# The second layer's sums of weights and of x^T: from GpSimd to the vector engine

## The chip, the cores and the metric

One NeuronCore of a Trainium2 chip runs the whole program. The metric is the device time of one execution in microseconds; the kernel before has a median of 953.41 us over three runs (953.21 to 955.58). Engines are called as the profile calls them: PE is TensorE's matrix multiply, PEld its weight load, DVE the vector engine, ACT the scalar engine, POOL GpSimd, SP the queue that issues the transfers.

## The reference, cut to what matters

```python
attn_out = windowed_attention(q, k, v)                 # 4 x 8 heads, 576 positions, width 64
x = attn_out.transpose(0, 2, 1, 3).reshape(2304, 512)
x = rational(x @ moe_w_in) @ moe_w_out                 # layer 1: 512 -> 2048 -> 512
h = x @ moe2_w_in                                      # layer 2: 512 -> 2048
g = where(h > 0, h, exp(min(h, 0)) - 1)
return g @ moe2_w_out                                  # 2048 -> 512
```

All is float32. The change touches layer 2 alone.

## The kernel before

The kernel keeps x transposed (tile `xT`) and runs attention, layer 1 and layer 2 one after the other. Layer 2 starts at about 551 us of the span. Each float32 operand of a product is split into a high part, rounded to the matmul's format by ACT (`hi_w`, `hi_op`, lines 870 and 905), and a low part, which DVE makes as the difference (`lo`, line 875); each product is three passes.

Layer 2 goes over three groups J of 768 tokens, and in each over 8 steps of 256 columns of d_ff: 24 steps q. Within a step, h of 2 x 2 blocks is made by seven block products instead of eight. They are called b11, b21, t2, t3, t1, t4 and b22 (`product`, line 918), and they need sums of blocks: four sums of weight blocks (`sum_w`, line 848, four instructions of 128x256 that read the tile `two` and write the two tiles `s`) and four sums of blocks of x^T (`sum_x`, line 896, two instructions of 128x384 each). DVE adds the seven products up into the four blocks of h (`added`, line 974, which reads the product m from PSUM), ACT and DVE make g from each block (lines 980, 984, 989, 1006 and 875), and PE multiplies g of the step before by w_out (`gemm2`, line 934). On PE a step is b11, b21, G0, t2, t3, G1, t1, G2, t4, b22, G3, where G are the four second products.

Sums of weights are made once, in the first group, for w = 0 to 7 (w is the step they belong to), stored in DRAM by SP (`keep_sums`, line 853) and loaded again in the other groups. w = 0 and w = 1 are summed by DVE, w = 2 to 7 by POOL. The two tiles `s` are the same for all w, so the sums of one w wait until the stores of the last one have landed and its low parts are made. The sums of x^T for J = 0 are made by DVE during layer 1; those for J = 1 and J = 2 by POOL, over the x rows of the group before.

Layer 2's order is not written by hand. `step` notes for each piece of work its engine, an estimated cost and what it needs; `in_order` lays the pieces out with those costs, by due times counted back from PE's fixed order, counting a transfer as landed 3500 ns behind its issue cost (1200 for a load of weight blocks), and every engine then runs its pieces in that order. The estimates of before are 3500 ns for a set of four weight sums on POOL, 1400 ns for one on DVE, and 2300 ns for two sums of x^T on POOL. An engine's real start is set by semaphores: POOL, with nothing else to do, starts a sum as soon as its data are there.

Of the kernel before, what the change touches and what calls it, by code (L numbers as in the profile page):

```python
# [44 lines left out]
def kernel(  # L45
# [13 lines left out]
    nc = tc.nc  # L59
# [150 lines left out]
    def cv_tile(shape, dtype, name, n=None):  # L210
        n = next(n_cv) if n is None else n
        return cv.tile(shape, dtype, tag=f"cv{n}", name=f"{name}{n}")
# [480 lines left out]
    def experts():  # L693
# [47 lines left out]
        OPS, XO, sums, G, sq, kept, low_part = {}, {}, {}, {}, {}, {}, {}  # L741
# [56 lines left out]
        def raw_ones(q):  # L798

            return [e for e in range(2) if q < NP2 and ("wo", KF + 2 * q + e) not in early_ones]  # L800

        def load_raw(q, e):
            key = ("wo", KF + 2 * q + e)
            SLOT[key] = SETS[q % 3]["EF"[e]]
            load_w(key)

        def load_wi(q):
            two[q] = t = at(q, "C", [P, 2, PC], F32, "two")
            for e in range(2):
                nc.sync.dma_start(out=t[:, e], in_=joined["wi", KF + q % NP2 * 2 + e])  # L810
# [6 lines left out]
        def load_wo(q, e):  # L817
            nc.sync.dma_start(out=both(e), in_=joined["wo", KF + q % NP2 * 2 + e])

        def scale_wo(q, e):  # L820
            key = ("wo", KF + 2 * q + e)
            T32[key] = both(e)
            nc.scalar.activation(out=both(e), in_=words(key)[1].bitcast(F32), func=AF.Copy, scale=2.0 ** -112)

        def join_wo(q, e):
            key = ("wo", KF + 2 * q + e)
            conv_shift(key)
            conv_or(key)
            conv_sign(key)
            del RAW[key]  # L830

        def keep_wo(q, e):
            key = ("wo", KF + 2 * q + e)
            joined[key] = d = dram.tile([P, PC], F32, name="joined_%s_%d" % key)
            nc.sync.dma_start(out=d, in_=T32[key])

        def sum_w(q, eng=nc.gpsimd, ns=range(4)):
            w = two[q]
            a11, a12, a21, a22 = [w[:, e, h * HC:(h + 1) * HC] for e in range(2) for h in range(2)]
            if 0 in ns:  # L840
                sq[q] = [cv_tile([P, 2, HC], F32, "s", n) for n in range(2)]
            s = sq[q]
            for n in ns:
                x, y, op = (
                    (a21, a22, ALU.add), (s[0][:, 0], a11, ALU.subtract), (a11, a21, ALU.subtract),
                    (a12, s[0][:, 1], ALU.subtract),
                )[n]
                eng.tensor_tensor(out=s[n // 2][:, n % 2], in0=x, in1=y, op=op)

        def keep_sums(w):  # L850
            kept[w] = [dram.tile([P, PC], F32, name=f"sums_{w}_{n}") for n in range(2)]
            for d, t in zip(kept[w], sq[w]):
                nc.sync.dma_start(out=d, in_=t.rearrange("p s c -> p (s c)"))

        def load_sums(w):
            sq[w] = [cv_tile([P, 2, HC], F32, "s", n) for n in range(2)]
            for d, t in zip(kept[w % NP2], sq[w]):
                nc.sync.dma_start(out=t.rearrange("p s c -> p (s c)"), in_=d)

        def hi_w(q, x):  # L860
            if x in "CD":
                src = sq[q]["CD".index(x)].rearrange("p s c -> p (s c)")
            elif x == "B":
                src = two[q][:, 1, HC:PC]
            elif x == "A":
                src = two[q][:, 0]
            else:
                src = pair[0][:, "EF".index(x)]
            OPS[q, x] = t = at(q, x, [P, 2, HC if x == "B" else PC], F32R, "op")
            nc.scalar.activation(out=t[:, 0], in_=src, func=AF.Copy)  # L870
            low_part[q, x] = (t[:, 1], src, t[:, 0])

        def lo(key, eng=nc.vector):
            out, src, hi = low_part.pop(key)
            eng.tensor_tensor(out=out, in0=src, in1=hi.bitcast(F32), op=ALU.subtract)  # L875

        def x_row(J, k, T):
            c0 = (2 * J + T) * TB
            return xT[:, k, c0:c0 + TB]

        def sum_x(J, n, eng=nc.gpsimd, ks=range(2)):

            if 0 not in ks:
                pass
            elif J == 0:
                nm = "_".join(map(str, t_slots[n]))
                t = wpool.tile([P, 2, TB], F32, tag=nm, name=f"t_{nm}")
                sums[J, n] = [t[:, k] for k in range(2)]
            else:
                sums[J, n] = [x_row(J - 1, k + 2 * (n // 2), n % 2) for k in range(2)]  # L890
            for k in ks:
                b11, b21, b12, b22 = [x_row(J, k + 2 * i, T) for T in range(2) for i in range(2)]
                x, y = (
                    (b12, b11), (b22, sums[J, 0][k]), (b22, b12), (b21, sums[J, min(n, 1)][k]),
                )[n]
                eng.tensor_tensor(out=sums[J, n][k], in0=x, in1=y, op=ALU.subtract)
# [63 lines left out]
        def step(key, engine, cost, fn, *needs):  # L960
            todo[key] = (engine, cost, fn, needs)
            if engine == "PE":
                pe_order.append(key)
# [71 lines left out]
        def weight_steps(w):  # L1035

            def part(x, cost_hi, cost_lo, *needs):
                step((w, "hi", x), "ACT", cost_hi, lambda: hi_w(w, x), *needs)
                step((w, "lo", x), "DVE", cost_lo, lambda: lo((w, x)), (w, "hi", x))

            if w == 0:
                step((w, "kept"), "SP", 1200, lambda: keep_sums(w))
            else:
                out_gone = [(w - 2, "out", T, t) for T in range(2) for t in range(NTT)]
                if w > 1:
                    step((w, "load"), "SP", 1200, lambda: load_wi(w), (w - 3, "t1"), (w - 3, "t2"))
                gone = [(w - 1, "lo", "C"), (w - 1, "lo", "D")]
                if w >= NP2:
                    step((w, "sum"), "SP", 1200, lambda: load_sums(w), *gone)
                else:  # L1050
                    eng, cost, at = (nc.vector, 1400, "DVE") if w == 1 else (nc.gpsimd, 3500, "POOL")
                    step((w, "sum"), at, cost, lambda: sum_w(w, eng), (w, "load"), *gone, (w - 1, "kept"))
                    step((w, "kept"), "SP", 1200, lambda: keep_sums(w), (w, "sum"))
                part("A", 520, 600, (w, "load"), (w - 3, "b11"), (w - 3, "b21"), *out_gone)
                part("B", 300, 340, (w, "load"), (w - 3, "t4"), *out_gone)
                part("C", 520, 600, (w, "sum"), (w, "lo", "A"), (w, "lo", "B"))
                part("D", 520, 600, (w, "sum"), (w - 3, "t3"), (w - 3, "b22"), *out_gone)
            for e, x in enumerate("EF"):
                gone = [(w - 2, "G", n) for n in ((0, 3), (1, 2))[e]]
                if e in raw_ones(w):  # L1060
                    if w > 0:
                        step((w, "raw", x), "SP", 600, lambda e=e: load_raw(w, e), *gone)
                    step((w, "scale", x), "ACT", 570, lambda e=e: scale_wo(w, e), (w, "raw", x), (w - 1, "lo", x),
                         (w - 1, "keep", x))
                    step((w, "words", x), "DVE", 1600, lambda e=e: join_wo(w, e), (w, "scale", x))
                    step((w, "keep", x), "SP", 600, lambda e=e: keep_wo(w, e), (w, "words", x))
                else:
                    step((w, "words", x), "SP", 600, lambda e=e: load_wo(w, e), (w - 1, "lo", x),
                         (w - 1, "keep", x), (w - NP2, "keep", x))
                part(x, 520, 600, (w, "words", x), *gone)  # L1070
# [9 lines left out]
        def x_sums(J, q):  # L1080

            used = [("xlo", J - 1, nm, k) for nm in ORDER for k in range(2)]
            for n in range(4):
                step(("sum", J, n), "POOL", 2300, lambda n=n: sum_x(J, n), *used, (q - 4 + n, "b11"),
                     *[("sum", J, i) for i in range(n)])

        def second(q):
# [32 lines left out]
            if p == NP2 - 1 and q + 1 < NQ:  # L1120
                x_sums(q // NP2 + 1, q)
                x_steps(q // NP2 + 1, ORDER, q)
# [165 lines left out]
```

## Time and profile before

| | value |
|---|---|
| median of 3 runs | 953.41 us (953.21 to 955.58) |
| profiled execution, its own time | 951.87 us |
| its span | 950.2 us |
| PE busy | 920.9 us (97%) |
| DVE busy | 818.8 us (86%) |
| ACT busy | 745.1 us (78%) |
| POOL busy | 248.6 us (26%) |

Busy times are sums over the whole span; the three stages have different limits, so a share of the span says little about layer 2. Matmul ends are modelled, so that the start of a product is a safer mark than its busy time. DVE instructions overlap a little: the next one starts some 0.08 us before the last one's recorded end, so that the distance from start to start is what an instruction costs a full engine.

### The profile page before, as it was taken

What the parts mean: (1) busy time and instruction counts of PE and PEld (TensorE: products, weight loads), DVE (VectorE), ACT (ScalarE), POOL (GpSimd) and SP (SyncE); (2) the same over time, 40 slices, a digit from 0 to 9 for tenths busy, and PEclk for the clock granted to TensorE, in tenths of its full rate; (3) what the DMA queues carried; (4) which work ended last, traced back from release to release, by engine and by line L of the source; (5) the groups of instructions that cost most, each with busy time, mean ns of one, the idle gap of its engine ahead of it and who ended that gap; (6) DMA issues with size and microseconds to landing.
All of it is one profiled execution on the core that took longest, in us unless ns stands there. A gap on an engine that the chain in (4) does not pass through costs nothing.

```text
span 950.2 us, 16856 instructions
## 1 busy us (share of the span) xinstructions
PE 920.9 (97%) x5494; PEld 839.0 (88%) x5494; DVE 818.8 (86%) x1890; ACT 745.1 (78%) x1635; POOL 248.6 (26%) x312
## 2 busy tenths in 40 slices
PE   7999998999999999999999999999999999999998
PEld 5766767999999999999999988878889898989897
DVE  5999998999999999999999999899987678787653
ACT  4999999889889889889888986656777566766553
POOL 4777772122222222222222225350310000000000
PEclk8999999999999999999999999999999999999999
DMA  6899943011231222222210034434344332443201
GB/s 165 207 236 242 235 135 95 1 34 34 84 100 51 84 83 68 84 67 86 82 46 28 26 120 125 142 122 152 104 140 149 100 100 68 162 141 96 78 1 67
DMA packets 112424, 98.36 MB, mean 104 GB/s; under 512 B 62800, under 2 KB 86096, under 8 KB 112336
## 3 DMA queue, kind: packets, MB, share of 16 engines
q1 hardware_dynamic: 112336, 97.29, 35.1%
q8 instruction: 43, 0.70, 0.3%
q14 instruction: 45, 0.37, 0.1%
HBM read 79.96 MB, written 17.30 MB: 102 GB/s over the span
## 4 chain that ended last, share of the span: by engine, by line
PE 63%; DVE 18%; ACT 14%; issue 4%; DMA 1%; POOL 0%; SPq 0%; DVEq 0%; ACTq 0%; POOLq 0%
PE acc L934 17%; PE h L260 15%; PE acc L705 15%; PE m L918 14%; ACT pT L441 2%; ACT pr_wo L515 2%; ACT pr_wi L515 2%; DVE ghi L301 2%; DVE qq L304 1%; DVE ee L322 1%; DVE ee L318 1%; DVE qq L313 1%; DVE h L321 1%; DVE op_wi L875 1%; DVE op_wo L875 1%
## 5 line engine op out<-in xcount | busy, mean ns | idle before, releaser
L260 PE MATMUL h<-xs,w_wi 128*128 128x384 f32 x1152 | 218.1, 335 | 1.3 <-ACT xs L235 0.8
L260 PEld LDWEIGHTS h<-xs,w_wi 128*128 128x128 f32 x1152 | 200.4, 188 | 4.2 <-DVE xs L236 2.4
L705 PE MATMUL acc<-ghi,w_wo 128*128 128x384 f32 x768 | 195.0, 334 | 0.0
L319 POOL TENSOR_TENSOR glo<-ee,rr 128x384 fp32r<-128x384 f32 x92 | 93.5, 1016 | 315.8 <-DVE ee L318 160.9
L705 PEld LDWEIGHTS acc<-ghi,w_wo 128*128 128x128 f32 x768 | 138.7, 188 | 0.0
L705 PE MATMUL acc<-glo,w_wo 128*128 128x384 f32 x384 | 128.7, 335 | 0.9 <-DVE glo L319 0.5
L934 PE MATMUL acc<-op_wo,ghi 128*128 128x512 f32 x288 | 89.6, 392 | 0.0
L307 ACT ACTIVATE rr<-qq,c_q 128x384 f32<-128x384 f32 x96 | 59.3, 618 | 38.5 <-DVE qq L304 37.7
L918 PE MATMUL m<-xo_wo,op_wi 128*128 128x384 f32 x336 | 77.1, 337 | 7.2 <-DVE ee L974 4.0
L918 PE MATMUL m<-xo_wi,op_wi 128*128 128x384 f32 x336 | 77.2, 337 | 0.0
L980 ACT ACTIVATE oo<-qq 128x384 f32<-128x384 f32 x24 | 12.6, 525 | 79.0 <-DVE qq L974 79.0
L705 PEld LDWEIGHTS acc<-glo,w_wo 128*128 128x128 f32 x384 | 72.1, 188 | 2.0 <-POOL glo L319 1.2
L918 PEld LDWEIGHTS m<-xo_wo,op_wi 128*128 128x128 f32 x336 | 60.4, 188 | 13.0 <-DVE qq L974 3.7
L290 ACT ACTIVATE oo<-h,a_sb 128x384 f32<-128x384 f32 x96 | 67.8, 706 | 4.6 <-DVE h L321 3.7
L293 ACT ACTIVATE ee<-h,a_sb 128x384 f32<-128x384 f32 x96 | 67.5, 703 | 0.0
L301 DVE TENSOR_TENSOR ghi<-ee,rr 128x384 fp32r<-128x384 f32 x96 | 53.6, 558 | 12.2 <-ACT oo L290 0.5
L322 DVE TENSOR_TENSOR ee<-ee,h 128x384 f32<-128x384 f32 x96 | 53.2, 555 | 10.0
L934 PEld LDWEIGHTS acc<-op_wo,ghi 128*128 128x128 f32 x288 | 53.5, 188 | 8.9
L918 PEld LDWEIGHTS m<-xo_wi,op_wi 128*128 128x128 f32 x336 | 60.5, 188 | 0.0
L304 DVE SCALAR_TENSOR_TENSOR qq<-h,b_abs,qa 128x384 f32<-128x384 f32 x92 | 55.9, 608 | 3.7 <-ACT qa L289 3.7
L974 DVE TENSOR_TENSOR ee<-ee,m 128x384 f32<-128x384 f32 x96 | 52.5, 547 | 5.2 <-PE m L918 5.1
L934 PE MATMUL acc<-op_wo,glo 128*128 128x512 f32 x144 | 57.0, 396 | 0.0
(203 smaller groups left out, 2175.1 us busy)
## 6 DMA issues: line engine op xcount, KB each, us to landing
pair<-joined_wo SPq DMA_DIRECT2D x43, 256.0 KB, 2.7
raw_wo<-in_moe_w_out_dram SPq DMA_DIRECT2D x20, 512.0 KB, 5.1
raw_wi<-in_moe_w_in_dram SPq DMA_DIRECT2D x16, 512.0 KB, 4.6
half<-in_moe_w_in_dram SPq DMA_DIRECT2D x32, 256.0 KB, 2.7
two_wo<-joined_wi SPq DMA_DIRECT2D x32, 256.0 KB, 2.9
s<-sums SPq DMA_DIRECT2D x32, 256.0 KB, 2.8
half<-in_moe_w_out_dram SPq DMA_DIRECT2D x22, 256.0 KB, 2.8
v<-in_v_dram SPq DMA_DIRECT2D x32, 128.0 KB, 3.2
```

The source lines that it names most:

```text
L260: nc.tensor.matmul(h, lhsT=WT["wi", f][:, SEL[wp], kk * P:(kk + 1) * P], rhs=x[xp][kk], start=(kk == 0 and n == 0), stop=(kk == KD - 1 and ...
L290: nc.scalar.activation(out=oo, in_=h2, func=AF.Identity, scale=a_sb[:, 3:4], bias=a_sb[:, 1:2])
L293: nc.scalar.activation(out=ee, in_=h2, func=AF.Identity, scale=a_sb[:, 2:3], bias=a_sb[:, 0:1])
L301: nc.vector.tensor_tensor(out=hi, in0=ee0, in1=rr0, op=ALU.mult)
L304: nc.vector.scalar_tensor_tensor(out=qq, in0=h2, scalar=b_abs[:, 1:2], in1=qa, op0=ALU.mult, op1=ALU.add)
L307: nc.scalar.activation(out=rr, in_=qq, func=AF.Ln, bias=c_q)
L319: (nc.gpsimd if c > 4 else nc.vector).tensor_tensor(out=low, in0=ee0, in1=rr0, op=ALU.mult)
L322: nc.vector.tensor_tensor(out=ee, in0=ee, in1=h, op=ALU.add)
L705: nc.tensor.matmul(acc_t[d], lhsT=WT["wo", f][:, SEL[wp], d * P:(d + 1) * P], rhs=gt[SEL[xp]], start=(f == 0 and n == 0), stop=(f == KF - ...
L918: nc.tensor.matmul(out, lhsT=w[:, SEL[wp], c0:c0 + P], rhs=XO[q // NP2, nm, k][:, SEL[xp]], start=(k == 0 and n == 0), stop=(k == 1 and n ...
L934: nc.tensor.matmul(acc_t[T, t], lhsT=gt[SEL[xp]][:, t * P:(t + 1) * P], rhs=w[:, SEL[wp]], start=(first and n == 0), stop=(last and n == 2),)
L974: nc.vector.tensor_tensor(out=t, in0=R[q, x], in1=M[q, m], op=ALU.add)
```

## The change

The six sets of weight sums (w = 2 to 7, 24 instructions of 128x256) and the sums of x^T for J = 1 and 2 (16 instructions of 128x384) are noted for DVE instead of POOL, with the costs of 1400 ns per set and 950 ns per pair. Their needs are unchanged. Since `in_order` plans all engines together, the new costs also shift neighbours.

```diff
-                    eng, cost, at = (nc.vector, 1400, "DVE") if w == 1 else (nc.gpsimd, 3500, "POOL")
-                    step((w, "sum"), at, cost, lambda: sum_w(w, eng), (w, "load"), *gone, (w - 1, "kept"))
+                    eng = nc.vector
+                    step((w, "sum"), "DVE", 1400, lambda: sum_w(w, eng), (w, "load"), *gone, (w - 1, "kept"))
...
-                step(("sum", J, n), "POOL", 2300, lambda n=n: sum_x(J, n), *used, (q - 4 + n, "b11"),
+                step(("sum", J, n), "DVE", 950, lambda n=n: sum_x(J, n, nc.vector), *used, (q - 4 + n, "b11"),
```

POOL's own order ended like this before: from the sums of w = 5 (tiles s_7959 and s_7960, of which the last row stands here) to the last sums of x^T.

```order
L848 TENSOR_TENSOR s_7960<-two_wo_7916,s_7959 128x256
L896 TENSOR_TENSOR xT<-xT 128x384 x2
L848 TENSOR_TENSOR s_8125<-two_wi_8083 128x256
L848 TENSOR_TENSOR s_8125<-s_8125,two_wi_8083 128x256
L848 TENSOR_TENSOR s_8126<-two_wi_8083 128x256
L848 TENSOR_TENSOR s_8126<-two_wi_8083,s_8125 128x256
```

Behind these stand two more sums of x^T, the four of w = 7, and then 12 of x^T in one row: the rest of J = 1 and all of J = 2. Now POOL has nothing in layer 2.

The DVE rows of step 1, around the sums of w = 2, before (L974 are the additions of products, L989 and L875 to `glo` and `rr` belong to g, L875 to `op_...` are low parts of weights):

```order
L974 TENSOR_TENSOR ee_7695<-ee_7672,m 128x384
L875 TENSOR_TENSOR op_wo_7644<-pair,op_wo_7644 128x512
L989 SCALAR_TENSOR_TENSOR h_7674<-h_7674,qq_7639 128x384
L875 TENSOR_TENSOR op_wi_7518<-two_wo_7456,op_wi_7518 128x256
L875 TENSOR_TENSOR op_wi_7681<-s_7632,op_wi_7681 128x512
L875 TENSOR_TENSOR glo_7705<-h_7674,ghi_7704 128x384
```

and now:

```order
L974 TENSOR_TENSOR ee_7684<-ee_7666,m 128x384
L989 SCALAR_TENSOR_TENSOR h_7668<-h_7668,qq_7633 128x384
L848 TENSOR_TENSOR s_7687<-two_wo_7456 128x256
L848 TENSOR_TENSOR s_7687<-s_7687,two_wo_7456 128x256
L848 TENSOR_TENSOR s_7688<-two_wo_7456 128x256
L848 TENSOR_TENSOR s_7688<-two_wo_7456,s_7687 128x256
L875 TENSOR_TENSOR op_wo_7638<-pair,op_wo_7638 128x512
L875 TENSOR_TENSOR glo_7694<-h_7668,ghi_7693 128x384
```

The four sums stand behind the first block's g, and two low parts of weights have moved behind them.

The DVE rows at the end of step 3, around the sums of w = 6 (tile two_wi is the load they read; the row that writes ee_8042 or ee_8051 is the addition of product b22), before:

```order
L875 TENSOR_TENSOR glo_8101<-oo,ghi_8100 128x384
L974 TENSOR_TENSOR ee_8051<-ee_8051,m 128x384
L989 SCALAR_TENSOR_TENSOR h_8112<-h_8112,ee_8063 128x384
L875 TENSOR_TENSOR op_wo_8134<-two_wi_8083,op_wo_8134 128x512
L989 SCALAR_TENSOR_TENSOR oo<-oo,ee_8051 128x384
```

and now:

```order
L875 TENSOR_TENSOR glo_8109<-oo,ghi_8108 128x384
L974 TENSOR_TENSOR ee_8042<-ee_8042,m 128x384
L848 TENSOR_TENSOR s_8125<-two_wi_8081 128x256
L848 TENSOR_TENSOR s_8125<-s_8125,two_wi_8081 128x256
L848 TENSOR_TENSOR s_8126<-two_wi_8081 128x256
L848 TENSOR_TENSOR s_8126<-two_wi_8081,s_8125 128x256
L989 SCALAR_TENSOR_TENSOR h_8111<-h_8111,ee_8055 128x384
L875 TENSOR_TENSOR op_wo_8131<-two_wi_8081,op_wo_8131 128x512
L989 SCALAR_TENSOR_TENSOR oo<-oo,ee_8042 128x384
```

The sums, and with them the wait for their load, now stand on DVE ahead of two rows of g. The sums of x^T stand on DVE as pairs: those of J = 1 one pair in each of steps 3 to 6, those of J = 2 one pair in each of steps 11 to 14. On SP the stores of the sums now wait for DVE; the stores of w = 3 stand one weight load earlier than before, and the load of w = 5 two stores and one weight load earlier.

## Rows read from the trace of the kernel before

**Rows 1.** Windows: us, busy us (instructions) by engine, clock, DMA.
```profile
551.00:568.00 17.00, 14.67 (x84) 14.06 (x83) 16.29 (x35) 14.19 (x31) 3.05 (x3) 1.00 0.30 104
568.00:692.00 124.00, 116.96 (x573) 102.77 (x572) 115.66 (x192) 81.53 (x167) 47.53 (x40) 1.00 0.40 126
692.00:935.00 243.00, 243.00 (x1209) 218.65 (x1208) 174.29 (x333) 154.00 (x311) 0.97 (x1) 1.00 0.32 100
```

**Rows 2.** Timeline of PE: start, length, instruction [idle before it, releaser].
```profile
567.66 0.77 PE L918 MATMUL m<-xo_wo,op_wi 128*128 128x384 f32 x3 [2.26 <-DVE ee L974]
...
576.11 0.69 PE L918 MATMUL m<-xo_wo,op_wo 128*128 128x384 f32 x3
...
593.90 0.79 PE L918 MATMUL m<-xo_wo,op_wo 128*128 128x384 f32 x3 [1.73 <-DVE ee L974]
...
642.36 0.79 PE L918 MATMUL m<-xo_wo,op_wi 128*128 128x384 f32 x3 [2.86 <-DVE qq L974]
...
683.56 0.79 PE L918 MATMUL m<-xo_wo,op_wi 128*128 128x384 f32 x3 [1.75 <-DVE ee L974]
...
695.17 0.69 PE L918 MATMUL m<-xo_wo,op_wo 128*128 128x384 f32 x3
...
710.87 0.69 PE L918 MATMUL m<-xo_wo,op_wi 128*128 128x384 f32 x3
```

**Rows 3.** Timeline of POOL, same columns.
```profile
588.46 1.08 POOL L848 TENSOR_TENSOR s<-two_wo 128x256 f32<-128x256 f32 x1 [3.70 <-DMA sums<-s]
589.62 1.07 POOL L848 TENSOR_TENSOR s<-s,two_wo 128x256 f32<-128x256 f32 x1
...
615.38 0.74 POOL L848 TENSOR_TENSOR s<-two_wi 128x256 f32<-128x256 f32 x1 [9.53 <-DMA two_wi<-joined_wi]
...
672.56 7.60 POOL L896 TENSOR_TENSOR xT<-xT 128x384 f32<-128x384 f32 x6 [31.98 <-DVE xo_wo L875]
```

**Rows 4.** Timeline of DVE while POOL works.
```profile
571.19 1.09 DVE L989 SCALAR_TENSOR_TENSOR h<-h,ee 128x384 f32<-128x384 f32 x1
...
588.86 1.23 DVE L875 TENSOR_TENSOR op_wo<-pair,op_wo 128x512 fp32r<-128x512 f32 x1
590.01 1.23 DVE L875 TENSOR_TENSOR op_wi<-two_wo,op_wi 128x512 fp32r<-128x512 f32 x1
...
592.31 1.07 DVE L989 SCALAR_TENSOR_TENSOR h<-h,qq 128x384 f32<-128x384 f32 x1
593.31 0.54 DVE L974 TENSOR_TENSOR ee<-qq,m 128x384 f32<-128x384 f32 x1
...
616.46 0.54 DVE L974 TENSOR_TENSOR ee<-ee,m 128x384 f32<-128x384 f32 x1
...
691.19 0.91 DVE L875 TENSOR_TENSOR g<-oo,g 128x384 fp32r<-128x384 f32 x1
```

**Rows 5.** Timeline of DVE while POOL is idle.
```profile
652.10 0.69 DVE L875 TENSOR_TENSOR op_wi<-s,op_wi 128x512 fp32r<-128x512 f32 x1
652.70 0.55 DVE L989 SCALAR_TENSOR_TENSOR h<-h,ee 128x384 f32<-128x384 f32 x1
...
654.61 0.55 DVE L875 TENSOR_TENSOR g<-h,g 128x384 fp32r<-128x384 f32 x1
655.08 0.42 DVE L875 TENSOR_TENSOR op_wi<-two_wo,op_wi 128x256 fp32r<-128x256 f32 x1
655.42 0.55 DVE L974 TENSOR_TENSOR qq<-qq,m 128x384 f32<-128x384 f32 x1
```

**Rows 6.** Line 974, 566 to 692 us: engine, tiles xcount: ns min/median/max, starts.
```profile
L974 DVE TENSOR_TENSOR ee<-ee,m x30: 539/544/555, 567.0 to 686.4; 128x384 f32<-128x384 f32 x30
```

**Rows 7.** Line 848, same columns: the sums that DVE already made.
```profile
L848 DVE TENSOR_TENSOR s<-two_wo x2: 417/419/421, 563.2 to 564.0; 128x256 f32<-128x256 f32 x2
```

**Rows 8.** Windows, columns of Rows 1: step 5 from its t1 to the next.
```profile
645.59:661.30 15.71, 15.71 (x79) 14.11 (x78) 14.72 (x29) 11.02 (x22) 0.00 (x0) 1.00 0.45 150
```

**Rows 9.** Tile two_wi: loads, time from issue to landing.
```profile
DMA to landing us min/median/max: 2.5/3.0/4.6
```

## The prediction

> **What bounds the kernel now.** I read the windows of layer 2 first. From 692 to 935 us PE is busy without a gap; from 568 to 692 us it is busy 116.96 of 124 us; the piece ahead of that, 551 to 568, has another 2.3 us idle [rows 1]. So layer 2 is bound by PE at its end, and in its first third by something that PE waits for. POOL's work in layer 2 lies in that third: 47.53 us busy, and almost nothing behind it.
>
> Next the timeline of PE, to see whom it waits for. Every idle piece over 0.15 us is ended by an addition on DVE, line 974; the three large ones behind 568 us start again at 593.90, 642.36 and 683.56, after 1.73, 2.86 and 1.75 us [rows 2]. Because a product that restarts is slow too, I measure the loss from start to start, by product t1. From step 8 (695.17) to step 9 (710.87) it is 15.70 us. From step 1 (576.11) to step 8 it is 119.06 us, where seven such steps make 109.90: **9.16 us are lost** [rows 2]. The wait of 2.26 us that ends at 567.66 lies ahead of POOL's first sum and ahead of the first DVE row that moves, so it stays.
>
> Then DVE in that third: 115.66 of 124 us busy, 93% [rows 1]. What fills it? Side by side with POOL's sums of 588.46 and 589.62 [rows 3], a low part of 128x512 at 588.86 takes 1.15 us to the next start, and line 989 at 592.31 takes 1.00 [rows 4]. With POOL idle the same forms take 0.60 (652.10 to 652.70), 0.47 for 128x384 (654.61 to 655.08), and 0.34 for 128x256 (655.08 to 655.42) [rows 5]. Additions that read a product from PSUM are not stretched: 30 of them lie between 539 and 555 ns [rows 6]. The stretched rows read two tiles of SBUF, and they lie where POOL works. Each of PE's three large gaps ends just behind such a stretch: the addition at 593.31 that PE's t1 of 593.90 waited for stands behind four stretched rows.
>
> **The change part by part.** *Removed: the stretch.* I went through the DVE rows from 568 to 692 us and took, for each row whose distance to the next start is over that of its form undisturbed, the difference. There are 30 rows, the first at 571.19, the last at 691.19 [rows 4], in nine groups: 1.64, 0.71, 2.18, 2.19, 0.63, 2.21, 3.68, 4.03 and 0.36, together **17.6 us**.
>
> *Added: the sums.* 24 instructions of 128x256 at 0.34 us are 8.2 us; DVE made such sums before in 417 to 421 ns each by its records [rows 7], and start to start that is the 0.34 of [rows 5]. 16 instructions of 128x384 at 0.47 are 7.5 us. Of these 15.7 us the eight for J = 2, 3.8 us, move out of the third: POOL began them at 672.56, in the same moment as DVE makes the low parts of x [rows 3], while the new order has them in steps 11 to 14, where DVE is busy 174.29 of 243 us and PE has no gap [rows 1]. They are hidden there; a pair costs 0.94 us and stands beside some 4 us of slack a step. So 12.0 us come into the third.
>
> *The sum on DVE.* 115.66 - 17.6 + 12.0 = 110.1 us. DVE's load falls by 5.6 us, although it gets all the sums, and the window that PE needs falls to 124 - 9.16 = 114.8 us. The load would then be 96% of the window. Is that few enough for no gap? The nearest row: in step 5 DVE is busy 14.72 of 15.71 us, 94%, with POOL idle, and PE has no gap [rows 8]. If 94% were the most that DVE can bear, the window would be 110.1 / 0.94 = 117.1 us and 2.3 us of the loss would stay; if it can be filled, none. I take the middle, **1.2 us that stay**, so a gain of 8.0 us.
>
> *Order.* The planner's costs (1400 and 950) now agree with 4 x 0.34 and 2 x 0.47, where POOL's 3500 and 2300 left out what they cost DVE. At the gap of 593.90: between the first addition of step 2 and the one that t1 waits for, the new order has six rows, 0.47 x 3 + 0.60 x 2 + 0.34 = 3.0 us; before there were six too, and the last four alone took 4.45 (588.86 to 593.31) [rows 4].
>
> *Waits.* The sums of w = 6 and 7 now wait for their load on DVE, and behind them stand the g rows of two blocks. The load of w = 6 landed by 615.38, when POOL started [rows 3]; the addition ahead of the sums on DVE started at 616.46 [rows 4], and both follow PE's step, so about 1.1 us of cover remain. The load's landing takes 3.0 us at the median and 4.6 at most [rows 9]; a late one would cost some 0.5 us each. The stores of the sums on SP wait for DVE now, with the loads of w_out's blocks queued behind them; those wait for low parts that DVE makes anyway. I cost both at nothing and keep up to 1 us for the range, inside the 2.3.
>
> *A rule that speaks against it.* The rows show DVE as 93% busy and POOL free for most of layer 2 [rows 1]. The Trainium skill, Perfetto Trace Analysis, section Optimizing Scalar/DVE Operations, says that where DVE is saturated, giving work to ScalarE or even GPSIMD may make sense, and adds that between GPSIMD and DVE it might not help, since they share a read port. By its first half the move goes the wrong way, and the time would be that of the third rival; the stretched rows are on the side of its second half.
>
> **The rivals.** *First: DVE becomes the bound.* Its idle time of before in the third, 124 - 115.66 = 8.3 us [rows 1], is waiting for ACT and PE; if all of it stays, the window is 110.1 + 8.3 = 118.4 us, the gain 5.6, and with a few waits of the sums some 4: about 949. For it: from its first addition to that of step 3, step 2 now holds 16 DVE rows of 0.47, ten of 0.60 and six of 0.34, 15.6 us, of the 15.70 that PE gives it. Against: idle time shrinks when there is a queue, and PE's gaps were not where DVE idled.
>
> *Second: the sums hold DVE up.* On POOL a wait for a load or a store harmed nobody (9.53 us at 615.38) [rows 3]. If each of the six sets holds DVE for the 1.6 us between a median landing and the longest [rows 9], 9.6 us go and nothing is won: about 953.8. Against: the planner counts 1200 + 3500 ns for a load, more than the longest.
>
> *Third, slower: the stretch isn't POOL's.* If something else that runs in the same moments stretched those rows, transfers for instance, DVE keeps its 17.6 us and gets 12.0 more: 127.7 us in a window of 124, so at least 3.7 us longer: 957.1. It decides for "slower" once less than 115.66 + 12.0 - 124 = 3.7 us of the stretch go away. Against: all 30 rows lie beside POOL instructions, and [rows 8] has more transfers than the mean of the third (150 against 126 GB/s) [rows 1] without any stretch.
>
> **How the numbers follow.** The profiled execution took 951.87 us, 1.67 more than its span, and the median of the runs 953.41; the difference of 1.54 is spread over the execution, and I take the gain from the median: 953.41 - 8.0 = **945.4 us**, for the profiled execution 943.9. Chances: the forecast, 944 to 947.5, 0.62; the first rival 0.18; the second 0.12; the third 0.08. The low end is the whole loss regained, 953.41 - 9.16 = 944.2, less 0.3 for the spread of the runs: 943.9. The high end takes in the first rival with some 2 us more of waits: 950.8. A measurement of this kernel can tell about 0.3% (2.9 us) from no change: faster by more is the forecast and most of the first rival, 0.76; within it the rest of that and the second, 0.16; slower 0.08.
>
> **What would show it.** Right: POOL has no rows behind 560 us; lines 875 and 989 keep to 0.60 and 0.47 us through 568 to 692; PE's t1 comes every 15.7 to 16 us from step 1 on; the wait of 2.26 us at 567.66 is still there; DVE is busy about 110 us in the 115 after 568. Wrong in the order of the rivals: DVE full and PE still waiting for line 974; rows of line 848 on DVE with idle time ahead of them that a transfer ends; rows of line 875 at 1.1 us with POOL idle. The step that I trust least is how much of the loss stays with DVE at 96%.

## The result, and the profile after

| | before | after |
|---|---|---|
| median | 953.31 us (952.39 to 955.58, 4 runs) | 943.40 us (942.24 to 944.09, 4 runs) |
| span of the profiled execution | 950.2 us | 942.0 us |
| PE / DVE / POOL busy | 920.9 / 818.8 / 248.6 us | 918.9 / 815.4 / 199.9 us |

The ratio is 0.9894, with a 95% interval of 0.9880 to 0.9909: **1.06% faster, by some 9.9 us (8.7 to 11.4)**. The forecast was 945.4 us, with 943.9 as the low end of its range; the measured time lies 2.0 us below the forecast and 0.5 us below the range.

First the windows of layer 2 that answer to [rows 1] (us, then busy us and instructions of PE, PEld, DVE, ACT and POOL, the granted clock, the DMA share, GB/s):

```profile
551.00:568.00 17.00, 15.34 (x87) 14.70 (x86) 16.29 (x36) 14.29 (x31) 3.05 (x3) 1.00 0.30 110
568.00:683.00 115.00, 114.31 (x568) 102.96 (x569) 111.05 (x228) 83.32 (x168) 0.00 (x0) 1.00 0.41 138
683.00:927.00 244.00, 244.00 (x1214) 219.65 (x1213) 176.72 (x340) 154.24 (x311) 0.00 (x0) 1.00 0.30 100
```

PE is busy in all of the first third but 0.69 us, which are the tail of the wait that was there before too. POOL is empty. DVE is busy 111.05 of 115 us, 96.6%, and has 36 instructions more, 32 of them the moved sums, in a window that is 9 us shorter: before, part of its busy time was rows that took longer than they do now. In the stretch behind it, from 683 us, PE is busy 244.00 of 244.00 us, so the sums for J = 2, which now stand there, cost nothing.

The timeline of PE (start, length, instruction, idle before it with its releaser), against [rows 2]:

```profile
568.68 0.76 PE L918 MATMUL m<-xo_wo,op_wi 128*128 128x384 f32 x3 [2.26 <-DVE ee L974]
...
577.11 0.68 PE L918 MATMUL m<-xo_wo,op_wo 128*128 128x384 f32 x3
...
592.82 0.69 PE L918 MATMUL m<-xo_wo,op_wo 128*128 128x384 f32 x3
...
687.06 0.69 PE L918 MATMUL m<-xo_wo,op_wo 128*128 128x384 f32 x3
...
702.76 0.69 PE L918 MATMUL m<-xo_wo,op_wi 128*128 128x384 f32 x3
```

From the t1 of step 1 (577.11) to that of step 8 (687.06) it is 109.95 us, seven steps of 15.71; before it was 119.06. The whole loss of 9.16 us is gone. The waits that were at 593.90, 642.36 and 683.56 have no row any more; of all PE's waits between 568 and 683 us one is left (engine, line, releaser: us, times, longest):

```profile
PE m L918 <- DVE ee L974: 2.3, 1, 2.3
```

The same by another measure, from the start of the first product of layer 2 to the start of the last row of second products (the view joins three matmuls in a row). Before:

```profile
551.37 0.68 PE L918 MATMUL m<-xo_wo,op_wo 128*128 128x384 f32 x3
...
945.62 0.84 PE L934 MATMUL acc<-op_wo,g 128*128 128x512 f32 x3
```

and after:

```profile
552.38 0.68 PE L918 MATMUL m<-xo_wo,op_wo 128*128 128x384 f32 x3
...
937.47 0.84 PE L934 MATMUL acc<-op_wo,g 128*128 128x512 f32 x3
```

394.25 us before, 385.09 after: **9.16 us**, again the loss to the hundredth. The first product itself stands 1.01 us later in this execution of after, although the change touches nothing ahead of layer 2; the granted clock, for one, was 0.91 there between 140 and 160 us, and 1.00 in before's execution. I call this measure the length of layer 2 below; it leaves out what varies ahead of layer 2.

DVE around the sums of w = 4 (timeline); before, PE waited 1.73 us here, until 593.90, behind four stretched rows [rows 4]:

```profile
592.23 0.69 DVE L875 TENSOR_TENSOR op_wo<-pair,op_wo 128x512 fp32r<-128x512 f32 x1
592.83 0.69 DVE L875 TENSOR_TENSOR op_wi<-two_wo,op_wi 128x512 fp32r<-128x512 f32 x1
593.43 0.42 DVE L848 TENSOR_TENSOR s<-two_wo 128x256 f32<-128x256 f32 x1
593.89 0.43 DVE L848 TENSOR_TENSOR s<-s,two_wo 128x256 f32<-128x256 f32 x1
594.23 0.42 DVE L848 TENSOR_TENSOR s<-two_wo 128x256 f32<-128x256 f32 x1
594.57 0.42 DVE L848 TENSOR_TENSOR s<-two_wo,s 128x256 f32<-128x256 f32 x1
594.90 0.55 DVE L974 TENSOR_TENSOR qq<-ee,m 128x384 f32<-128x384 f32 x1
```

Each low part of 128x512 is back at 0.60 us from start to start, where it took 1.15. The four sums take 1.47 us, 593.43 to 594.90, without idle time ahead of them. One detail had not been counted: the first sum takes 0.46 to the next start, so a set is 1.47 us and not the 4 x 0.34 = 1.36 of the forecast. The second sum reads what the first has just written, which is the likely reason; no run tests it.

### The profile page after: what moved, and what is told of

Read it like the earlier page. It is cut to its first block, busy times and chain, and to the rows that moved or that the text cites. A ratio compares the mean times of both kernels' runs of the same rounds, so it can differ in the third digit from the quotient of the medians.

```text
span 942.0 us, 16811 instructions
## 1 busy us (share of the span) xinstructions
PE 918.9 (98%) x5494; PEld 840.0 (89%) x5494; DVE 815.4 (87%) x1930; ACT 747.9 (79%) x1635; POOL 199.9 (21%) x272
## 4 chain that ended last, share of the span: by engine, by line
PE 71%; DVE 15%; ACT 11%; issue 2%; DMA 1%; SPq 0%; DVEq 0%; ACTq 0%
PE acc L934 21%; PE m L918 18%; PE h L260 14%; PE acc L705 14%; ACT pT L441 2%; ACT pr_wi L515 2%; DVE ghi L301 2%; DVE ee L322 2%; ACT pr_wo L515 2%; DVE qq L304 2%; DVE ee L318 1%; DVE qq L313 1%; DVE h L321 1%; PE s_ps L474 1%; ACT cvt L134 1%
## 5 line engine op out<-in xcount | busy, mean ns | idle before, releaser
L974 DVE TENSOR_TENSOR ee<-ee,m 128x384 f32<-128x384 f32 x96 | 52.7, 550 | 5.1 <-PE m L918 4.8
```

The lines of the kernel that those rows point to most:

```text
L974: nc.vector.tensor_tensor(out=t, in0=R[q, x], in1=M[q, m], op=ALU.add)
```

## The experiments

The runs, with the median, its ratio to the kernel before on the same chip (951.7 to 953.3 us), and the length of layer 2 in each one's profiled execution:

| run | what it is | median us | ratio (95%) | layer 2, us |
|---|---|---|---|---|
| before | | 953.31 | | 394.25 |
| after | | 943.40 | 0.9894 (0.9880 to 0.9909) | 385.09 |
| e1 | order of after, POOL makes the sums | 950.96 | 0.9978 (0.9961 to 0.9995) | 395.99 |
| e2 | order of before, DVE makes them | 945.92 | 0.9934 (0.9919 to 0.9949) | 388.96 |
| e3 | only the sums of x^T on DVE | 944.94 | 0.9923 (0.9909 to 0.9938) | 387.61 |
| e4 | only the sums of weights on DVE | 953.62 | 1.0009 (0.9998 to 1.0020) | 395.50 |
| e5 | after, and POOL reads again | 964.13 | 1.0120 (1.0102 to 1.0139) | 407.12 |
| e6 | after, and POOL only writes | 944.34 | 0.9907 (0.9888 to 0.9926) | 386.69 |
| e7 | after, sums of w = 2 to 4 twice | 946.65 | 0.9933 (0.9917 to 0.9950) | 390.03 |
| e8 | after, sums of w = 5 to 7 twice | 945.63 | 0.9925 (0.9902 to 0.9948) | 387.95 |
| e9 | after, start of layer 2 planned anew | 943.14 | 0.9911 (0.9898 to 0.9925) | 386.51 |
| e10 | after once more, beside e9 | 942.37 | 0.9911 (0.9892 to 0.9931) | 385.11 |

The theory: two-input DVE instructions are stretched while POOL reads SBUF, PE waits for the additions behind them, and the change takes the stretch away. Its rivals: the gain comes from the new order, which the planner makes with costs that now are true; or the stretch is made by something else that runs in the same moments; or it is DVE's load alone that counts.

### The engine and the order apart (e1, e2)

e1 keeps the plan of after, and lets POOL carry it out:

```diff
-                    eng = nc.vector
+                    eng = nc.vector if w == 1 else nc.gpsimd
...
-                step(("sum", J, n), "DVE", 950, lambda n=n: sum_x(J, n, nc.vector), *used, ...
+                step(("sum", J, n), "DVE", 950, lambda n=n: sum_x(J, n), *used, ...
```

> The new order of all engines is kept, but the 40 sums are executed by POOL, as before the change. If the stretch of DVE's rows beside POOL is the cause (my theory), some 17 us of stretch come back in the first third of layer 2 and the time is that of the kernel before, 951 to 956 us. If the gain came from the order that the planner makes with the new costs, it stays near 943.4 us.

e2 is the reverse, the plan of before with DVE as the engine:

```diff
-                    eng, cost, at = (nc.vector, 1400, "DVE") if w == 1 else (nc.gpsimd, 3500, "POOL")
+                    eng, cost, at = (nc.vector, 1400, "DVE") if w == 1 else (nc.vector, 3500, "POOL")
...
-                step(("sum", J, n), "POOL", 2300, lambda n=n: sum_x(J, n), *used, ...
+                step(("sum", J, n), "POOL", 2300, lambda n=n: sum_x(J, n, nc.vector), *used, ...
```

> The order planned with the old POOL costs is kept, but the 40 sums are executed by DVE where POOL's would have been issued. Stretch theory: DVE is rid of its 17.6 us and gets 12.0, so the time is 943.5 to 946.5 us, the rest being what a badly placed row costs. Order theory: near the kernel before, 951 us or more.

Measured: e1 950.96 (948.19 to 953.99, 10 runs), e2 945.92 (945.32 to 946.66, 4 runs). With the order of before, the move of the work alone gives 953.04 - 945.92 = 7.1 us; with POOL at work, the order alone gives 953.04 - 950.96 = 2.1 us. The two make 9.2, and the difference from e2 to after is 2.5. So **the larger part, some 7 us, is the engine, and 2 to 2.5 us are the order**; by the intervals of the ratios the first lies between 4.9 and 7.7 us, the second between 0.5 and 3.7. PE's waits behind 568 us say the same of the order: 7.0 us in before, 5.0 in e1. e2 came as expected; e1 came just under its 951 to 956, since the order was worth more than I had thought.

e1's length in the table, 395.99 us, is over that of before in spite of this. Its profiled execution, 953.47 us, is the second longest of its ten, and the granted clock fell behind three of its waits (0.76, 0.50 and 0.76 over the 3 us behind 567.55, 640.91 and 683.60), which the last section comes back to.

PE's timeline in e1:

```profile
640.91 1.33 PE L918 MATMUL m<-xo_wo,op_wi 128*128 128x384 f32 x3 [3.10 <-DVE qq L974]
```

and DVE ahead of the addition that it waits for, in e1:

```profile
635.88 1.50 DVE L875 TENSOR_TENSOR op_wi<-two_wo,op_wi 128x512 fp32r<-128x512 f32 x1
637.31 1.22 DVE L875 TENSOR_TENSOR op_wo<-two_wo,op_wo 128x256 fp32r<-128x256 f32 x1
638.45 0.42 DVE L137 TENSOR_SCALAR raw_wi<-raw_wi 128x512 int32<-128x512 int32 x1
...
640.31 0.55 DVE L974 TENSOR_TENSOR qq<-qq,m 128x384 f32<-128x384 f32 x1
```

POOL made sums of x^T until 638.25; up to then the rows take 1.43 and 1.14 to the next start, where 0.60 and 0.34 would do, and then the stretch ends. The gap that stood at 593.90 is not there in e1: that one the order took away. The gaps at 640.91 and 683.60 are the old ones. In e2, with no stretch, two small ones are left on PE:

```profile
638.20 0.80 PE L918 MATMUL m<-xo_wo,op_wi 128*128 128x384 f32 x3 [0.44 <-DVE qq L974]
...
657.93 0.79 PE L918 MATMUL m<-xo_wo,op_wi 128*128 128x384 f32 x3 [0.60 <-DVE ee L974]
```

### Which of the sums (e3, e4)

e3 leaves the six sets of weight sums as they were before the change (on POOL, 3500 ns), e4 the sums of x^T (on POOL, 2300 ns); each moves only the other kind. e3 undoes the first hunk of the diff, e4 the second.

> One half of the change alone: sums of x^T on DVE, sums of weights w = 2 to 7 on POOL. About 5.2 of the 18.4 us of stretch were beside the weight sums alone, and PE's gap at 593.90 (2.1 us from start to start) is theirs: some 3 us of the gain are lost, 945 to 948.5 us.

> The other half alone: sums of weights on DVE, the 16 sums of x^T on POOL, where nothing stands ahead of them now, so that those of J = 1 start at once, at about 563 us, when DVE is fullest. At some 0.9 us of stretch for each, 7 us come there and 4 to 5 us for J = 2 at about 665 us: 948 to 953 us. If only the number of instructions that move counted (16 of 40), it would be about 947.

Measured: e3 944.94 (944.14 to 945.76), all but 1.5 us of what after has; e4 953.62 (952.60 to 954.19, 10 runs), nothing at all. Neither was quite in its range. (The 18.4 us in e3's expectation mean the stretch that the prediction counts as 17.6.) The 24 sums of weights beside DVE cost PE 0.70 us in e3:

```profile
593.49 0.80 PE L918 MATMUL m<-xo_wo,op_wo 128*128 128x384 f32 x3 [0.70 <-DVE ee L974]
```

e4's miss teaches more. The order that the planner makes for it has POOL start all sums of J = 1 the moment it is free. POOL, PE and DVE in e4:

```profile
559.51 10.16 POOL L896 TENSOR_TENSOR xT<-xT 128x384 f32<-128x384 f32 x8
```

```profile
573.23 1.30 PE L918 MATMUL m<-xo_wo,op_wi 128*128 128x384 f32 x3 [8.16 <-DVE ee L974]
```

```profile
562.50 1.36 DVE L875 TENSOR_TENSOR xo_wi<-xT,xo_wi 128x384 fp32r<-128x384 f32 x1
563.78 1.50 DVE L875 TENSOR_TENSOR op_wi<-two_wo,op_wi 128x512 fp32r<-128x512 f32 x1
```

The wait of 2.26 us that before and after share has become 8.16. DVE was late there already, and ten microseconds of POOL in that place cost PE 5.9 us. So it is not only how many instructions POOL runs, but where: before, the sums of J = 1 began on POOL behind 600 us. The sums of J = 2 stayed beside the low parts of x at 673 us, and the old wait there is in e4 too (2.02 us, ending at 684.44). e3 has the counterpart: there 25 us of POOL's sums, spread from 568 to 633 us, cost PE the 0.70 us above. Since the six us are a matter of place, e3 and e4 do not add up to after and are not the shares of the two kinds.

### Reading or writing (e5, e6)

Both keep the kernel after as it is, and give POOL 40 instructions of the old shapes besides, planned with the old costs, whose results nobody uses: e5 subtracts the same tiles into a spare one, e6 writes zeros into it.

```diff
+        def spare_w(w, write_only):
+            t = cv_tile([P, PC], F32, "spare", 2)
...
+                if write_only:
+                    nc.gpsimd.memset(t[:, 0:HC], 0.0)
+                else:
+                    nc.gpsimd.tensor_tensor(out=t[:, 0:HC], in0=x, in1=y, op=ALU.subtract)
...
+                        step((w, "spare"), "POOL", 3500, lambda: spare_w(w, False), (w, "load"), *gone)
```

> The changed kernel, with POOL making 40 subtractions of the same sizes from the same tiles into a spare tile that nobody reads (additional work, the output is not touched). Stretch theory: DVE keeps the sums and gets some 17 us of stretch on top, 128 us of work in a window of 115: 953 to 960 us, slower than the kernel before. If transfers or something else stretched DVE's rows: 943.4 us.

> As e5, but the 40 instructions of POOL only write (a fill of the spare tile, 128x256 and 128x384). If a busy POOL is enough to hold DVE, rows of lines 875 and 989 beside it are stretched and the time rises by 2 us or more; if it is POOL's reading, nothing is stretched and the time stays 943.4 us within 1 us. By the Trainium skill, SBUF - State Buffer, section Who interferes with whom, a DVE instruction with two SBUF inputs contends with a GpSimd instruction that reads SBUF and not with one that only writes.

Measured: e5 964.13 (963.34 to 965.64), 20.7 us above after; e6 944.34 (942.38 to 944.96), after's time within the spread. In these two kernels low parts are line 893, additions 992, products 936 and line 989 is 1007. POOL and then DVE in e5:

```profile
644.67 15.27 POOL L866 TENSOR_TENSOR spare<-xT 128x384 f32<-128x384 f32 x12
```

```profile
648.54 1.48 DVE L893 TENSOR_TENSOR op_wi<-two_wo,op_wi 128x512 fp32r<-128x512 f32 x1
649.95 1.21 DVE L893 TENSOR_TENSOR op_wo<-two_wo,op_wo 128x256 fp32r<-128x256 f32 x1
651.08 1.22 DVE L137 TENSOR_SCALAR raw_wi<-raw_wi 128x512 int32<-128x512 int32 x1
...
655.02 0.54 DVE L992 TENSOR_TENSOR qq<-qq,m 128x384 f32<-128x384 f32 x1
```

The low parts take 1.41 and 1.13 us instead of 0.60 and 0.34; the addition at 655.02, which has one of its inputs in PSUM, keeps its 0.54, amid the same POOL work. Between 568 and 692 us PE has eight waits in e5, 17.4 us in all, the longest ending in this row:

```profile
655.61 1.33 PE L936 MATMUL m<-xo_wo,op_wi 128*128 128x384 f32 x3 [7.26 <-DVE qq L992]
```

It is more than before had, and more than I expected, because these sums need no tile `s` and so start earlier: at 560.41, where the wait of the first step grows from 2.26 to 5.98 us, and with twelve in one row from 644.67.

POOL and DVE in e6:

```profile
559.49 5.88 POOL L855 MEMSET spare<- 128x256 f32 x16
...
570.29 5.67 POOL L864 MEMSET spare<- 128x384 f32 x12
```

```profile
561.77 0.69 DVE L893 TENSOR_TENSOR op_wi<-two_wo,op_wi 128x512 fp32r<-128x512 f32 x1
...
572.43 0.68 DVE L893 TENSOR_TENSOR op_wi<-two_wo,op_wi 128x512 fp32r<-128x512 f32 x1
573.03 0.55 DVE L1007 SCALAR_TENSOR_TENSOR oo<-oo,ee 128x384 f32<-128x384 f32 x1
573.50 0.55 DVE L893 TENSOR_TENSOR glo<-h,ghi 128x384 fp32r<-128x384 f32 x1
```

Beside POOL's writes the same forms keep 0.60 and 0.47. No two-input row of DVE between 559.5 and 576 us is over 0.69 us. The writes ran earlier than the sums once did, since nothing holds them back, and they were shorter (0.47 us each for 128x384); but DVE has hardly a pause there either, and e4 had POOL's reads in the same place: the low part that takes 0.69 us at 561.77 here took 1.50 at 563.78 there. **It is POOL's reading that stretches DVE's two-input rows.** After, e5 and e6 issue the same transfers, so the third rival is out. The Trainium skill, SBUF — State Buffer, section Who interferes with whom, states just this: a DVE instruction with two SBUF inputs contends with a GpSimd instruction that reads SBUF, and not with one that only writes. e5 and e6 agree, with 1.41 against 0.60 us for the same form.

### How full DVE may be (e7, e8)

e7 makes the sums of w = 2 to 4 twice on DVE, e8 those of w = 5 to 7: each adds 12 instructions, about 4.1 us, to one half of the third.

```diff
-                    step((w, "sum"), "DVE", 1400, lambda: sum_w(w, eng), (w, "load"), *gone, (w - 1, "kept"))
+                    again = 2 if w in (2, 3, 4) else 1
+                    step((w, "sum"), "DVE", 1400, lambda: [sum_w(w, eng, again * tuple(range(4)))], (w, "load"), *gone,
+                         (w - 1, "kept"))
```

> The changed kernel with the four sums of w = 2, 3 and 4 made twice on DVE (the second time over the same values), 12 rows more, 4.1 us, in the stretch from 568 to 611 us where DVE has no idle time; the order is kept. If DVE at 96% is at its limit, PE loses 2 to 4 us: 945.5 to 947.5. If PE's next product always has a few us of cover, nothing: 943.4.

> The same 12 rows, 4.1 us, but for w = 5, 6 and 7: where DVE had about 4 us of idle time between 611 and 683 us. The idle time takes most of it: 943.4 to 945 us. If the mean load over the third decided, it would be the same as e7.

Measured: e7 946.65 (945.59 to 947.22), 3.2 us above after and in its range; e8 945.63 (944.61 to 947.35), 2.2 above, somewhat over its range. The two differ by less than their intervals. PE waits again. In e7:

```profile
598.23 0.79 PE L918 MATMUL m<-xo_wo,op_wi 128*128 128x384 f32 x3 [2.15 <-DVE ee L974]
```

and in e8:

```profile
639.01 0.79 PE L918 MATMUL m<-xo_wo,op_wi 128*128 128x384 f32 x3 [1.52 <-DVE qq L974]
```

Behind the first step PE's waits come to 2.46 us in e7 and 1.84 in e8, of the 4.1 us that were added. So after's DVE, 96.6% busy, has room for some two microseconds in either half, and no more. In e7 the granted clock fell behind the wait as well (0.66 between 598.3 and 601.3 us), so its 3.2 us, and its length of 390.03, are not the waits alone. The first rival described a real limit; the change stops just short of it.

### The wait that stays (e9, e10)

The wait of 2.26 us ahead of b11 of step 1 is there in before, in after and in most of the runs. The planner lets PE begin at 0 and DVE at 5500 ns; in after's trace DVE's first addition of layer 2 (559.85) stands 7.5 us behind PE's first product (552.38). e9 lets DVE begin 2.6 us later, and drops the need of the first step's t3 for that addition:

```diff
-            multiply(q, "t3", (q, "h11"))
+            multiply(q, "t3", *[(q, "h11")] * (q > 0))
...
-            free = {"PE": 0, "ACT": 3400, "DVE": 5500, "POOL": 0, "SP": 0}
+            free = {"PE": 0, "ACT": 3400, "DVE": 8100, "POOL": 0, "SP": 0}
```

> The kernel after the change, with the start of layer 2 told as the trace shows it: DVE's first addition is planned at 8100 ns instead of 5500 (in the trace it stands some 2.6 us behind its planned place against PE), and the third product of the first step no longer counts as needing it. The order of DVE then has the addition h21 of step 0 ahead of the sums of w = 1. If the wait of 2.26 us ahead of b11 of step 1 is no more than this order, it goes, and perhaps 0.4 us come back at the first second product, which then waits for the low part of g: 1.5 to 2.3 us less than after (941.1 to 941.9 beside 943.4), and up to 1.6 more where the half clock that followed the wait in some executions stays away too. If DVE is the bound there (it is 96% busy, and full without a gap up to 611 us), the wait only turns up a step later: 943.4 again, and another row of line 974 releases PE between 570 and 610 us.

> The kernel after the change once more, unchanged, on the same chip as the run before it, so that the two are compared like with like: 943.4 within a microsecond. If the half clock behind the wait at 568 us is a matter of the single execution, its runs spread over some 1.6 us.

Measured: e9 943.14 (942.60 to 944.24), e10, which is after itself, 942.37 (941.60 to 946.62) on the same chip: no gain. e10's six runs spread over 5.0 us where 1.6 were expected, five of them over 2.5. PE in e9:

```profile
560.75 0.79 PE L918 MATMUL m<-xo_wo,op_wi 128*128 128x384 f32 x3 [1.54 <-DVE qq L974]
...
567.22 0.77 PE L918 MATMUL m<-xo_wo,op_wi 128*128 128x384 f32 x3 [0.97 <-ACT ghi L1006]
...
569.06 0.79 PE L918 MATMUL m<-xo_wo,op_wi 128*128 128x384 f32 x3 [0.53 <-DVE ee L974]
```

One wait of 2.26 us has become three of 3.04 in all. An addition that stood first on DVE in after (`qq<-qq,m` at 559.85) stands third in e9, at 560.15, and it is the one that t1 waits for at 560.75; what is taken from one product is missed by the next. Some 0.7 us of that wait are stretch again: ahead of the addition a low part takes 1.15 us to the next start (558.07 to 559.22) instead of 0.47, beside POOL's last row of layer 1 (557.86). So e9 shows that this order does not pay, not that none does.

## Why the prediction was right, and where it was not

The time came out below the range. The mechanism held; two sizes did not, the 1.2 us that were to stay and the 0.3 us allowed for the spread of the runs.

**The bound** was read rightly: PE waiting for line 974, 9.16 us between the t1 of step 1 and of step 8. The length of layer 2 fell by just that.

**The stretch** was read rightly, from rows alone: e5 brings it back, e6 shows that it takes POOL's reads, and e2 that most of the gain comes without the new order.

**The sum on DVE** was 110.1 us; it is 111.05 in the 115 us after 568. Six sets of 1.47 us instead of 1.36 are 0.7 of the difference; I did not trace the rest.

**The step that failed is the term of 1.2 us that were to stay.** The forecast took 94%, from [rows 8], as a possible most for DVE, and the middle between that and none. It is the step that the prediction trusted least, and it should have been zero: at 96.6% PE has no wait at all behind 568.68. A busy share of a step in which nobody waited is a load that was seen to do, not a limit, and half of 2.3 us had no row behind it. Nor does the share tell who waits: from 569 to 683 us DVE is busy 107.31 of 114 us in e2, 94%, and PE waits 1.04 us there; in e9 it is busy 111.85, 98%, and PE waits for nothing behind 569.06. What decides, as far as these runs show, is whether the addition that PE wants next stands early enough in DVE's order. The order has a price of its own, 2 to 2.5 us by e1 and e2, which the forecast named but gave no term; with the old one, e2, DVE makes the same sums and PE waits 0.44 and 0.60 us. And the limit is near: 4.1 us more in one half of the third bring 3.2 or 2.2 us back.

**The low end of the range** failed too, by the 0.3 us allowed for the spread of the runs. With the whole loss regained, 953.41 - 9.16 gives 944.25, and 943.40 was measured; the other 0.85 us are not in layer 2, and no run ties them to the change. The runs of before spread over 3.2 us and those of after over 1.9, and a good part of that lies ahead of layer 2: its first product starts between 550.34 (e7) and 552.38 us (after) in the profiled executions, 2.0 us apart, while its length is 385.09 and 385.11 us in two executions of after. The medians of before on the chips used here lie between 951.72 and 953.34. Beside e10 the same change gained 951.72 - 942.37 = 9.35 us, which taken from 953.41 gives 944.06, inside the range. So the last 0.5 us are spread between measurements, and 943.9 was too tight for it.

**The waits**: DVE has no idle time ahead of any row of line 848 on w = 2 to 7; the second rival did not come. The set of w = 6 starts at 614.45 on DVE, right behind an addition, where POOL had been waiting for its load.

**What was to stay**, stayed: the 2.26 us at the first step, unmoved, and the one attempt to remove it, e9, only moved it. **The third rival** is refuted by e5 and e6. **The first rival** is what e7 and e8 look like.

**The rule that speaks against the change** (the Trainium skill, Perfetto Trace Analysis, section Optimizing Scalar/DVE Operations), that work may be given away where DVE is saturated, did not carry here: work that takes DVE 15.7 us by the prediction's count stretched DVE's rows by 17.6 us when POOL had it, more than the work itself. It is the second half of that advice, that it might not help between these two engines, that the runs bear out.

## What to carry to other kernels

Before work is given to GpSimd, or taken back, look at the VectorE rows beside it: the price of GpSimd's work was here the stretch of VectorE's instructions that read their inputs from SBUF, not GpSimd's own time. Count it by comparing the distance between starts of one form with GpSimd at work and with GpSimd idle; if the sum is over what VectorE would need for the work, and somebody waits for VectorE there, move the work. The place matters as much as the sum: 25 us of GpSimd's sums cost PE 0.70 us in e3, and 10 us of them, in the first step, 5.9 us in e4. And judge a nearly full engine by whether its next awaited instruction comes in time, in its order, not by its busy share.

## What the runs showed of the hardware

*The stretch takes a one-input instruction as well.* Line 137, a TENSOR_SCALAR, reads one SBUF tile of 128x512 int32. With POOL idle it takes 0.42 us (the row at 638.45 in e1), beside POOL's reads 1.22 (the row at 651.08 in e5). I had expected it of two-input rows alone, but before has such a row too, 1.25 us at 638.48, and it is one of the 30 that the prediction counted. The additions, which read PSUM, kept their time beside it; their commonest form in e5 (line 992; ns min/median/max, starts):

```profile
L992 DVE TENSOR_TENSOR ee<-ee,m x28: 542/547/553, 561.8 to 684.1; 128x384 f32<-128x384 f32 x28
```

The Trainium skill, SBUF — State Buffer, section Who interferes with whom, counts this operation among those that can enter a mode with two ports and so can contend; the rows agree with that, but no run here shows which mode it ran in.

*POOL's rows can be longer beside DVE, too.* An instruction of 128x256 takes 0.74 us at some places and 1.19 at others, one of them 3.55. From POOL's timeline in e1:

```profile
592.20 0.74 POOL L848 TENSOR_TENSOR s<-two_wo 128x256 f32<-128x256 f32 x1 [5.03 <-DVE op_wi L875]
...
595.06 1.19 POOL L848 TENSOR_TENSOR s<-two_wo,s 128x256 f32<-128x256 f32 x1
...
600.25 3.55 POOL L848 TENSOR_TENSOR s<-two_wo 128x256 f32<-128x256 f32 x1 [4.00 <-DVE op_wo L875]
```

POOL's times are rough, so I only read from it that POOL can pay as well. Beside the row of 3.55 us DVE's five rows that start between 600.51 and 602.65, all with two inputs in SBUF, kept their 0.55 and 0.68 us: not every row of DVE beside a row of POOL is stretched.

*A wait of PE can cost more than itself.* Behind some of PE's waits the granted clock was at half, the level of 1.2 GHz, for some 3 us. Windows of e6 and of e3 right behind the wait of 2.27 us, and of after behind its 2.26 (same columns as above), one fence each:

```profile
567.00:570.00 3.00, 2.66 (x11) 2.69 (x12) 2.80 (x6) 2.84 (x7) 2.54 (x9) 0.70 0.27 83
```

```profile
567.00:570.00 3.00, 3.00 (x10) 3.00 (x11) 2.44 (x5) 2.27 (x7) 1.55 (x1) 0.53 0.16 61
```

```profile
568.00:571.00 3.00, 2.31 (x13) 2.35 (x14) 3.00 (x7) 2.89 (x7) 0.00 (x0) 1.00 0.26 87
```

The same wait, and the clock falls in e1, e2, e3 and e6, not in before, after, e7, e8 and e10. In e6, which has no other wait behind it, layer 2 is 386.69 us long against after's 385.09, so the fall costs 1.6 us; without it, at the same price, e2 would be 2.3 us longer than after and e3 0.9. Behind the 3.10 us of e1 it fell as well (0.50 between 641 and 644 us), and the 2.86 us of before left it at full speed. That is a part of the difference between runs of one kernel, and a reason to compare medians rather than two profiles. What decides whether it falls is left open.
